# A linear-attention and MLP kernel on one core: the low part of the weights made by an accumulating DMA, and the plan's costs and start times set anew

## The chip, the cores and the metric

The kernel runs on one core of a Trainium2 chip. The metric is the device time of one execution in microseconds; before the change it is 558.08 us, the median of three runs (557.09 to 559.31). The core has five engines that run beside each other: TensorE (PE in the profile; its weight loads are shown apart as PEld), VectorE (DVE), ScalarE (ACT), GpSimd (POOL) and SyncE (SP), which here only issues DMAs. Each engine works through its own instructions in the order in which the program gives them.

## What is computed

```python
def _attn_ref(r, k, v, w, u):                    # B, H, S, D = 4, 8, 768, 48
    for t in range(S):
        cur = np.einsum('bhd,bhe->bhde', u[None] * kt, vt)
        y[:, :, t] = np.einsum('bhd,bhde->bhe', rt, state + cur)
        state = wt[:, :, :, None] * state + np.einsum('bhd,bhe->bhde', kt, vt)

def _moe_ref(x, w_in, w_out):                    # 3072 tokens, 384 -> 2048 -> 384
    h = x @ w_in
    g = np.where(h > 0.0, h, np.exp(np.minimum(h, 0.0)) - 1.0)
    return g @ w_out
```

A recurrent attention over 768 time steps, for 4 batches and 8 heads, feeds an MLP with an ELU between its two products. The MLP's weights are given in float64; the kernel gets them as pairs of 32-bit words.

## The kernel before

**Tiling.** Time is cut into 6 chunks of 128 steps. A *unit* is one chunk of one batch: 24 units, numbered i = 4 x chunk + batch. The MLP of a chunk takes its 4 units together, 512 columns, and goes through 16 *steps* f of 128 hidden columns each.

**A unit's attention.** Loads of w, k, r, v (L338) and, from unit 8 on, rk; two scans on DVE (es L344, gs L354); products r_hat and k_hat on DVE (L358, L361); the diagonal (by TensorE and ACT for the first 8 units, pd L385 and md L389, then am L396; by POOL and DVE for the others, L368, L371, L375, L403); the scores on TensorE (s, L413), masked by DVE (mk, L416); the value pass on TensorE (v, L443, tile pa_y), which needs the state; its result is split into a high and a low part, xh on ACT (L449) and xl on DVE (L453). For the next chunk's state the unit's k is transposed (t, L421), copied (kt, L425), multiplied with v (u, L460, tile pa_u) and added to the state by DVE (up, L468).

**A weight step.** For each f, two loads of 384 KB (w_in and w_out, L482) go to a raw buffer. ACT scales the upper words into a buffer wg (a, L487); DVE clears bits of the upper words (cand, L495) and merges both words into wg (cb L499, cc L503): wg now holds the weights in float32. ACT rounds them to the high part w_h (wh, L506), and DVE subtracts w_h from wg to get the low part w_l (wl, L509). There are two wg buffers, so the a of step f + 2 waits for the wl of step f. All 16 steps are converted once and stay in SBUF for all chunks.

**The MLP of a step.** Each product is the sum of three: w_h with xh, w_h with xl, w_l with xh. g1 is 9 matmuls (L227 to L229, three of each kind), then Relu and Exp on ACT (r1 L233, r2 L236), ELU on DVE (stt, L239), the split into gh (ACT, L243) and gl (DVE, L247), and g2, 9 matmuls into three accumulators (L256 to L258). A step may be cut into two half steps of 256 columns: for the first FH[c] steps of a chunk, the halves for batches 0 and 1 come first, then the halves for batches 2 and 3, and then the whole steps. After a chunk, its result is copied out and stored (L269, L270).

**The order.** A planner written out in the kernel (class Plan) makes the order of all engines' instructions. Each piece of work has an engine, an assumed cost (COST), what it must come after, and the buffers that it takes (SLOTS, hold). Backward from due times each gets a latest time ("late"); forward, a model of the engines picks, whenever an engine is free, the ready piece with the smallest latest time. The due times come from BEGINS, the assumed beginning of each chunk's MLP: step n of chunk c has its time t at BEGINS[c] + n x pace, with pace = (BEGINS[c+1] - BEGINS[c]) / 16; its g1 is due at t + 2.12 and its g2 at t + 2 x pace + 2.12. A buffer that is taken (three slots each for k, r and v, for four units of a chunk) holds a load back, but does not move the latest time of the work that frees it. A chunk's loads may not be planned before BEGINS[c] - LEAD. Only the order goes to the chip, where semaphores keep the dependences; the assumed costs do not.

Of the kernel before, what the change touches and what calls it, by code (L numbers as in the profile page):

```python
# [19 lines left out]
P = 128  # L20
# [12 lines left out]
FH = (6, 6)  # L33
# [23 lines left out]
def WLE(f):  # L57
    return "DVE"
# [15 lines left out]
class Plan:  # L74
# [15 lines left out]
    def order(self):  # L90
# [23 lines left out]
        ready = {e: [] for e in ("PE", "DVE", "ACT", "POOL", "SP")}  # L114
# [5 lines left out]
        server = 0.0  # L120
# [5 lines left out]
        while len(order) < len(ts):  # L126
            moved = False
            for e in ready:
# [33 lines left out]
                end = now + t["dur"]  # L162
                busy[e] = end
# [48 lines left out]
def mlp(nc, w_h, w_l, ps_acc, ps_h, ml, po, dst, last=False):  # L212
# [49 lines left out]
    def out(m):  # L262
# [13 lines left out]
def rwkv_elu_kernel(ctx, tc, wkr, rk, vp, u, uz, gkrw, gv, gu, w_in, w_out, out):  # L276
# [207 lines left out]
    def conv_a(f):  # L484
        g = stg.tile([P, 2, NK, P], U32, tag="wg", name="wg", bufs=2)
# [24 lines left out]

    def guard():
# [17 lines left out]
    for u_ in units:  # L529
        i, c, b = u_["i"], u_["c"], u_["b"]  # L530
        early = max(0.0, BEGINS[c] - LEAD) if c > 0 else 0.0
        for n, kb in (("w", 232), ("k", 229), ("r", 229), ("rk", 393), ("v", 262)):
            if n == "rk" and i < ND:
                continue
# [8 lines left out]
        if i < ND:  # L543
# [4 lines left out]
            add(("md", i), "ACT", K["md"], lambda u_=u_: diag_out(u_), [("pd", i)])  # L548
            add(("sp", i), "ACT", K["spa"], lambda u_=u_: spread_act(u_), [("md", i), ("const",)])
        else:  # L550
            e1, e2 = ENG(i)
            for n, e, fn, dep in (("rk", e1, r_k, [("ld_rk", i)]), ("rku", e2, r_k_u, [("rk", i), ("ub",)])):
                add((n, i), e, K[n if e == "DVE" else "p" + n],
                    lambda u_=u_, fn=fn, e=e: fn(u_, nc.vector if e == "DVE" else nc.gpsimd), dep, lock=True)
            add(("dg", i), "DVE", K["dg"], lambda u_=u_: diag(u_), [("rku", i)])
            add(("sp", i), "POOL", K["sp"], lambda u_=u_: spread(u_), [("dg", i)], lock=True)
# [16 lines left out]
    for f in range(NF):  # L573
# [10 lines left out]
        e = WLE(f)  # L584
        add(("wl", f), e, K["wl" if e == "DVE" else "pwl"], lambda f=f, e=e: conv_l(f, nc.vector if e == "DVE" else nc.gpsimd), [("wh", f)], lock=True)
# [29 lines left out]
    for u_ in units:  # L615
        i, c = u_["i"], u_["c"]
        for n, users in dict(w=["es", "gs"], k=["s", "t"], r=["s", "v"], rk=["dg"], v=["v", "u"]).items():
            hold(n, ("ld_" + n, i), [(x, i) for x in (users if n != "k" else users + ["kh"])])
        hold("eg", ("es", i), [("fl", i), ("rh", i), ("kh", i)] + [("pc", i)] * (c > 0))
        hold("md", ("md", i) if i < ND else ("dg", i), [("sp", i)])  # L620
        if i < ND:
# [16 lines left out]
    add(("guard",), "PE", 0.3, guard, [("fl", i) for i in range(NU)], due=BEGINS[-1] + 20)  # L638
# [127 lines left out]
```

## Time and profile before

| | us |
|---|---|
| median of three runs | 558.08 |
| the profiled execution | 556.87 |
| its span, first to last instruction | 554.8 |
| TensorE busy | 519.8 |
| DVE busy | 362.5 |
| ACT busy | 285.6 |
| POOL busy | 69.9 |

The page of the profile gives, for one execution, the busy time of each engine, the span in 40 equal slices (a digit is the busy share in tenths), and groups of instructions by line, with their count, busy time, mean duration in ns, and the idle time of the engine before them with what ended it. PEclk is the share of TensorE's full clock that the chip granted. Other views used here are a table of stretches (length, then the busy time of each engine with its instruction count, the granted clock, the DMA engines' busy share and GB/s), the chain of work that ended last in order of time, the waits of an engine for another, and the instructions in order of time. Matmuls overlap in the profile, so that the sum over groups is more than TensorE's busy time.

### The profile page before, as it was taken

Reading aid. Unit: us, or ns where it says so; the run is one execution under the profiler, and the core shown is the slowest. Engines: PE = TensorE matmul, PEld = TensorE weight load, DVE = VectorE, ACT = ScalarE, POOL = GpSimd, SP = SyncE. Lnnn points to the kernel's source line nnn. Section 1 sums busy time; section 2 is a strip of 40 time slices with the busy share of each in tenths; the row PEclk is TensorE's granted clock in tenths of the full one; section 3 lists DMA queues with packets and bytes.
Section 4 is the critical chain, followed back from the end, with each engine's and each line's share of the span. In section 5 each row is a group of like instructions: output and inputs, shape, how many; then the busy total and the mean of one; then the engine's idle time right before and its main releaser. Section 6 shows DMA issues by size and latency. Waiting matters only on the chain.

```text
span 554.8 us, 10007 instructions
## 1 busy us (share of the span) xinstructions
PE 519.8 (94%) x4065; PEld 430.3 (78%) x4065; DVE 362.5 (65%) x565; ACT 285.6 (51%) x558; POOL 69.9 (13%) x72
## 2 busy tenths in 40 slices
PE   5875999999999999999999999998799999999993
PEld 5765898889998887787878788876578878888882
DVE  6899999998796375369377335987596345333331
ACT  3668587687665443455443445643274432534441
POOL 1000000000240011215002300704530001000000
PEclk9977999999999999999999999999699999999998
DMA  8863574034410036211036200226520011100001
GB/s 267 250 199 120 156 234 168 1 87 144 122 60 2 0 90 192 59 55 36 0 91 201 69 0 18 74 91 209 153 70 1 0 37 38 58 0 1 0 1 61
DMA packets 26739, 47.36 MB, mean 85 GB/s; under 512 B 2752, under 2 KB 9280, under 8 KB 26688
## 3 DMA queue, kind: packets, MB, share of 16 engines
q1 hardware_dynamic: 26688, 46.66, 27.3%
q8 instruction: 34, 0.56, 0.4%
q14 instruction: 17, 0.14, 0.1%
HBM read 41.93 MB, written 4.72 MB: 84 GB/s over the span
## 4 chain that ended last, share of the span: by engine, by line
PE 83%; DVE 7%; DMA 3%; issue 3%; ACT 2%; SPq 1%; DVEq 0%; ACTq 0%
PE acc L256 12%; PE ph L227 12%; PE ph L229 11%; PE ph L228 11%; PE acc L257 11%; PE acc L258 11%; PE pa_y L443 6%; PE pa_s L413 4%; PE pa_u L460 2%; DMA v<-in_vp_dram 1%; PE pa_d L385 1%; PE pa_t L421 1%; DMA ubd<-in_uz_dram 1%; DVE gl L247 1%; DVE am L416 1%
## 5 line engine op out<-in xcount | busy, mean ns | idle before, releaser
L239 DVE SCALAR_TENSOR_TENSOR m<-m,ph 128x512 f32<-128x512 f32 (+1 forms) x108 | 67.1, 624 | 106.2 <-ACT m L236 105.9
L227 PE MATMUL ph<-xh,w_h 128*128 128x512 f32 (+1 forms) x324 | 123.2, 380 | 3.6 <-ACT w_h L506 1.6
L233 ACT ACTIVATE m<-ph 128x512 f32<-128x512 f32 (+1 forms) x108 | 59.3, 549 | 124.0 <-PE ph L229 120.8
L229 PE MATMUL ph<-xh,w_l 128*128 128x512 f32 (+1 forms) x324 | 121.0, 373 | 1.9 <-DVE w_l L509 1.9
L256 PE MATMUL acc<-gh,w_h 128*128 128x512 f32 (+1 forms) x325 | 122.0, 375 | 0.0
L228 PE MATMUL ph<-xl,w_h 128*128 128x512 f32 (+1 forms) x324 | 121.1, 374 | 0.2
L257 PE MATMUL acc<-gl,w_h 128*128 128x512 f32 (+1 forms) x325 | 120.2, 370 | 0.0
L258 PE MATMUL acc<-gh,w_l 128*128 128x512 f32 (+1 forms) x325 | 120.0, 369 | 0.0
L247 DVE TENSOR_TENSOR gl<-m,gh 128x512 fp32r<-128x512 f32 (+1 forms) x108 | 70.8, 658 | 35.1 <-ACT gh L243 34.8
L243 ACT CAST gh<-m 128x512 fp32r<-128x512 f32 (+1 forms) x108 | 61.4, 570 | 49.9 <-DVE m L239 43.4
L227 PEld LDWEIGHTS ph<-xh,w_h 128*128 128x128 f32 x324 | 62.2, 192 | 17.8 <-DVE m L239 3.0
L229 PEld LDWEIGHTS ph<-xh,w_l 128*128 128x128 f32 x324 | 62.1, 192 | 13.4 <-DVE w_l L509 2.4
L256 PEld LDWEIGHTS acc<-gh,w_h 128*128 128x128 f32 x325 | 61.4, 189 | 12.7 <-issue 1.0
L228 PEld LDWEIGHTS ph<-xl,w_h 128*128 128x128 f32 x324 | 62.3, 192 | 11.4 <-DVE xl L453 0.8
L258 PEld LDWEIGHTS acc<-gh,w_l 128*128 128x128 f32 x325 | 61.4, 189 | 11.3
L257 PEld LDWEIGHTS acc<-gl,w_h 128*128 128x128 f32 x325 | 61.4, 189 | 11.3 <-DVE gl L247 0.3
L236 ACT ACTIVATE m<-m 128x512 f32<-128x512 f32 (+1 forms) x108 | 63.1, 584 | 3.1
L403 POOL TENSOR_SCALAR_AFFINE_SELECT am<-md 128x512 f32<-128x512 f32 x32 | 29.2, 934 | 221.7 <-PE pa_y L443 156.2
L416 DVE COPY_PREDICATED am<-upper,pa_s 128x512 f32<-128x512 uint32 x48 | 32.8, 737 | 13.0 <-PE pa_s L413 11.9
L368 POOL TENSOR_TENSOR rk<-rk 128x384 f32<-128x384 f32 x16 | 18.3, 1147 | 171.9 <-DMA rk<-in_rk_dram 171.9
L413 PE MATMUL pa_s<-r,k 48*128 48x128 f32 x384 | 31.9, 304 | 7.7 <-issue 6.4
L413 PEld LDWEIGHTS pa_s<-r,k 48*128 48x128 f32 x384 | 26.9, 204 | 13.4 <-issue 9.9
(61 smaller groups left out, 504.4 us busy)
## 6 DMA issues: line engine op xcount, KB each, us to landing
v<-in_vp_dram SPq DMA_DIRECT2D x24, 256.0 KB, 3.1
rk<-in_rk_dram SPq DMA_DIRECT2D x16, 384.0 KB, 3.7
w<-in_wkr_dram SPq DMA_DIRECT2D x24, 226.2 KB, 4.8
k<-in_wkr_dram SPq DMA_DIRECT2D x24, 224.0 KB, 3.1
r<-in_wkr_dram SPq DMA_DIRECT2D x24, 224.0 KB, 5.1
out_dram<-o SPq DMA_DIRECT2D x17, 256.0 KB, 2.1
wrawx<-in_w_in_dram SPq DMA_DIRECT2D x10, 384.0 KB, 3.9
wrawx<-in_w_out_dram SPq DMA_DIRECT2D x10, 384.0 KB, 4.5
```

Source lines behind the costliest of these rows:

```text
L227: nc.tensor.matmul(ph, w_h[:, f, 0, k], xh[:, k, :], start=(k == 0), stop=False)
L228: nc.tensor.matmul(ph, w_h[:, f, 0, k], xl[:, k, :], start=False, stop=False)
L229: nc.tensor.matmul(ph, w_l[:, f, 0, k], xh[:, k, :], start=False, stop=(k == NK - 1))
L233: act(s["m"], s["ph"], AF.Relu, scale=-1.0)
L236: act(s["m"], s["m"], AF.Exp, scale=-1.0)
L239: stt_(s["m"], s["m"], -1.0, s["ph"], ALU.add, ALU.max)
L243: nc.scalar.copy(s["gh"], s["m"])
L247: nc.vector.tensor_tensor(s["gl"], s["m"], s["gh"].bitcast(F32), ALU.subtract)
L256: nc.tensor.matmul(a_, w_h[:, f, 1, m], s["gh"][:, s_], start=(f == 0 and lo == 0), stop=False)
L257: nc.tensor.matmul(a_, w_h[:, f, 1, m], s["gl"][:, s_], start=False, stop=False)
L258: nc.tensor.matmul(a_, w_l[:, f, 1, m], s["gh"][:, s_], start=False, stop=(f == NF - 1 and q == parts - 1))
L413: nc.tensor.matmul(pa[q][:, p], u_["k"][rs, p, :], u_["r"][rs, p, :], start=True, stop=True)
```

## The change

The low part of a weight step was wg - w_h on DVE. For the 12 steps in WLD, ACT now writes the negated, rounded wg into w_l (conv_n), and a DMA issued from POOL's queue adds wg to it in place (conv_d). Steps 0, 8, 11 and 15 keep DVE's subtraction. In the plan, the landing is a piece of work of its own on an assumed engine NET, with 4.0 us (WDL). A wg buffer is now held until w_l has landed and w_h is written.

The plan's other inputs change too. COST has new values. BEGINS and LEAD are new. FH was 6, 6 (half steps in chunks 0 and 1) and is now 4, 5, 0, 5. On TensorE the model adds 0.2 us (SWITCH) where the kind of work changes, and 3.9 us (STAY) to the latest time of work that would change between the kinds in MODES (s, v, u, pd) and all others. Each value pass of a chunk comes after the one of the batch before it. One of the two halves of the last output is issued from ACT's queue. The rest renames (DIAG and SPREAD say which engine makes the diagonal, as ND and ENG did, with the same assignment).

```diff
-FH = (6, 6)
+FH = (4, 5, 0, 5, 0, 0)
...
-COST = dict(es=1.5, gs=1.4, pc=0.2, pd=0.6, md=0.22, spa=2.4, rh=0.62, kh=0.62, rk=0.48, rku=0.48, prk=1.1, prku=1.1, dg=0.5, mk=0.7, up=0.7, sc=0.5, xl=0.48,
-            cand=0.5, cv=0.9, wl=0.9, pwl=1.9, stt=0.6, gl=0.64, fl=1.4, kt=0.5, xh=0.46, a=0.87, wh=0.8, r1=0.58, r2=0.6, gh=0.6,
-            sp=1.7, s=1.15, t=0.5, v=1.75, v0=1.1, u=0.5, g=2.12, out=0.6)
+COST = dict(es=1.2, gs=1.45, rh=0.61, kh=0.61, rk=0.48, rku=0.48, prk=1.0, prku=1.1, dg=0.47, mk=0.64, up=0.73, sc=0.47, xl=0.48,
+            pc=0.1, pd=0.45, md=0.1, spa=2.35, cand=0.5, cv=0.87, wl=0.87, pwl=1.9, wn=0.73, wd=1.0, stt=0.6, gl=0.6, fl=1.16, kt=0.43,
+            xh=0.43, a=0.81, wh=0.73, r1=0.56, r2=0.54, gh=0.52, sp=1.57, s=0.88, t=0.37, v=1.55, v0=0.9, u=0.37, g=2.1, out=0.5)
...
-BEGINS = (20.6, 125.1, 205.2, 299.0, 400.1, 445.7, 557.5)
+BEGINS = (19.3, 145.5, 209.8, 321.6, 420.1, 430.6, 535.4)
 SOON = 0.0
-LEAD = 70.0
-ND = 8
+STAY = 3.9
+SWITCH = 0.2
+MODES = dict(s=1, v=2, u=3, pd=4)
+WLD = (1, 2, 3, 4, 5, 6, 7, 9, 10, 12, 13, 14)
+WDL = 4.0
+LEAD = 96.4
+DIAG = ["PE"] * 8 + ["POOL"] * 16
+SPREAD = ["ACT"] * 8 + ["POOL"] * 16
...
-                    u = (t["late"], rank[k])
+                    u = (t["late"] + (STAY if e == "PE" and (k[0] in MODES) != (mode in MODES) else 0.0), rank[k])
...
                 end = now + t["dur"]
+                if e == "PE":
+                    end += SWITCH * (MODES.get(mode, 0) != MODES.get(k[0], 0))
+                    mode = k[0]
...
-            nc.sync.dma_start(dst[m * P:(m + 1) * P, s_], o[:, m, s_])
+            (nc.scalar if last and m == NK - 1 and q == 0 else nc.sync).dma_start(dst[m * P:(m + 1) * P, s_], o[:, m, s_])
...
+    def conv_n(f):
+        act(w_l[:, f], raws[f][1].bitcast(F32), AF.Copy, scale=-1.0)
+
+    def conv_d(f):
+        nc.gpsimd.dma_start(w_l[:, f].bitcast(F32), raws[f][1].bitcast(F32), accum_op=ALU.add)
...
+        if b:
+            after.append(("v", i - 1))
         add(("v", i), "PE", K["v" if c else "v0"], lambda u_=u_: value(u_), after)
...
-        e = WLE(f)
-        add(("wl", f), e, K["wl" if e == "DVE" else "pwl"], lambda f=f, e=e: conv_l(f, nc.vector if e == "DVE" else nc.gpsimd), [("wh", f)], lock=True)
+        if f in WLD:
+            add(("wn", f), "ACT", K["wn"], lambda f=f: conv_n(f), [("cc", f)])
+            add(("wd", f), "POOL", K["wd"], lambda f=f: conv_d(f), [("wn", f)])
+            add(("wl", f), "NET", WDL, lambda: None, [("wd", f)])
+        else:
+            add(("wl", f), "DVE", K["wl"], lambda f=f: conv_l(f, nc.vector), [("wh", f)], lock=True)
...
-        hold("wg", ("a", f), [("wl", f)])
+        hold("wg", ("a", f), [("wl", f), ("wh", f)])
...
-    add(("guard",), "PE", 0.3, guard, [("fl", i) for i in range(NU)], due=BEGINS[-1] + 20)
+    add(("guard",), "PE", 0.3, guard, [("fl", i) for i in range(NU)], due=BEGINS[-2] + 15)
```

More of the change, by code (lines that the diff above doesn't have):

```diff
@@ L113, in order @@
         free = lambda p, n: not any(ring[p][1][(ring[p][0] + x) % len(ring[p][1])] for x in range(n))
-        ready = {e: [] for e in ("PE", "DVE", "ACT", "POOL", "SP")}
+        ready = {e: [] for e in ("PE", "DVE", "ACT", "POOL", "SP", "NET")}
         count = {k: len(t["after"]) for k, t in ts.items()}
@@ L119, in order @@
         locked = {"DVE": 0.0, "POOL": 0.0}
-        server = 0.0
+        server, mode = 0.0, None
         turn = {p: list(q) for p, q in self.queue.items()}
@@ L548, in rwkv_elu_kernel @@
             add(("md", i), "ACT", K["md"], lambda u_=u_: diag_out(u_), [("pd", i)])
+        else:
+            e = DIAG[i]
+            for n, fn, dep in (("rk", r_k, [("ld_rk", i)]), ("rku", r_k_u, [("rk", i), ("ub",)])):
+                add((n, i), e, K[n if e == "DVE" else "p" + n],
+                    lambda u_=u_, fn=fn, e=e: fn(u_, nc.vector if e == "DVE" else nc.gpsimd), dep, lock=True)
+            add(("md", i), "DVE", K["dg"], lambda u_=u_: diag(u_), [("rku", i)])
+        if SPREAD[i] == "ACT":
             add(("sp", i), "ACT", K["spa"], lambda u_=u_: spread_act(u_), [("md", i), ("const",)])
         else:
[L551 to L556, printed above, removed]
+            add(("sp", i), "POOL", K["sp"], lambda u_=u_: spread(u_), [("md", i)], lock=True)
         add(("s", i), "PE", K["s"], lambda u_=u_: score(u_), [("rh", i), ("kh", i), ("sp", i)])
@@ L616, in rwkv_elu_kernel @@
         i, c = u_["i"], u_["c"]
-        for n, users in dict(w=["es", "gs"], k=["s", "t"], r=["s", "v"], rk=["dg"], v=["v", "u"]).items():
+        for n, users in dict(w=["es", "gs"], k=["s", "t"], r=["s", "v"], rk=["md"], v=["v", "u"]).items():
             hold(n, ("ld_" + n, i), [(x, i) for x in (users if n != "k" else users + ["kh"])])
         hold("eg", ("es", i), [("fl", i), ("rh", i), ("kh", i)] + [("pc", i)] * (c > 0))
-        hold("md", ("md", i) if i < ND else ("dg", i), [("sp", i)])
-        if i < ND:
+        hold("md", ("md", i), [("sp", i)])
+        if DIAG[i] == "PE":
             hold("rk", ("rkc", i), [("pd", i)])
```

9 lines of the change are left out of this document (4 added, 5 removed).

## The prediction

> **What bounds the kernel now.** I read the page's shares and slices first, then a table of stretches, then the waits and the order of time inside the bad stretches.
>
> ```profile
> span 554.8 us, 10007 instructions
> PE 519.8 (94%) x4065; PEld 430.3 (78%) x4065; DVE 362.5 (65%) x565; ACT 285.6 (51%) x558; POOL 69.9 (13%) x72
> ...
> PE   5875999999999999999999999998799999999993
> ...
> DVE  6899999998796375369377335987596345333331
> ...
> PEclk9977999999999999999999999999699999999998
> ```
>
> TensorE is the bound almost everywhere; two dents stand in its row (slices 1 to 4, and 27 and 28), and both have a dent in the granted clock. The first lies where DVE is at 9. The table of stretches gives sizes (busy us and instruction count by engine, then clock, DMA share, GB/s):
>
> ```profile
> 0.00:20.00 20.00, 13.84 (x80) 12.76 (x84) 14.50 (x24) 10.89 (x27) 2.31 (x8) 1.00 0.95 284
> 20.00:70.00 50.00, 38.65 (x410) 34.30 (x403) 46.19 (x76) 32.86 (x73) 0.00 (x0) 0.86 0.52 167
> 70.00:110.00 40.00, 40.00 (x205) 33.82 (x204) 39.47 (x59) 29.21 (x48) 0.00 (x0) 1.00 0.40 134
> ...
> 160.00:376.00 216.00, 214.21 (x1625) 172.40 (x1629) 136.15 (x209) 103.17 (x185) 35.80 (x33) 1.00 0.22 65
> 376.00:400.00 24.00, 18.43 (x272) 14.44 (x265) 14.55 (x24) 5.77 (x12) 11.43 (x11) 0.79 0.64 198
> 400.00:545.00 145.00, 145.00 (x898) 117.05 (x898) 67.46 (x102) 67.76 (x117) 8.66 (x9) 1.00 0.07 21
> ```
>
> Two stretches lose time. 20 to 70 us: 11.4 us of idle TensorE and 0.14 x 50 = 7.0 us of withheld clock, 18.4 in all, with DVE busy 46.2 of 50. 376 to 400 us: 5.6 idle and 0.21 x 24 = 5.0 clock, 10.6 in all, with no engine full. Elsewhere TensorE is busy throughout, so work taken from DVE after 70 us buys nothing by itself.
>
> The first loss. The chain passes through DVE here; its longest hole is put down to "issue", but DVE's own rows (the first and last of them here) run through it without a gap, because the third and fourth batch's scans and products must be done before the next scores:
>
> ```profile
> 43.92 6.38 issue
> ...
> 41.98 2.35 DVE L344 TENSOR_TENSOR_SCAN eg<-w,reset 112x516 f32<-112x516 f32 x2
> 44.25 0.93 DVE L499 SCALAR_TENSOR_TENSOR wg<-wg,wrawx 128x768 uint32<-128x768 uint32 x1
> 45.21 0.96 DVE L503 SCALAR_TENSOR_TENSOR wg<-wrawx,wg 128x768 uint32<-128x768 uint32 x1
> ...
> 50.12 0.68 DVE L358 TENSOR_TENSOR r<-r,eg 112x512 f32<-112x512 f32 x1
> ```
>
> So in this stretch a microsecond off DVE is about a microsecond off the path.
>
> The second loss is loads that come late for unit 19, the last of chunk 4:
>
> ```profile
> 377.95 0.60 PE L421 MATMUL pa_t<-ident,k 112*128 112x112 f32 x4
> 378.59 2.87 DMA k<-in_wkr_dram
> 382.00 0.56 PE L460 MATMUL pa_u<-v,kt 128*48 128x48 f32 x16
> 383.85 0.63 SPq L338 DMA_DIRECT2D v<-in_vp_dram  x1
> 391.39 1.94 PE L443 MATMUL pa_y<-am,v 128*32 128x128 f32 x32 [4.34 <-DMA v<-in_vp_dram]
> ```
>
> k and v have three slots for four units of a chunk. k(19) may load only after the transpose of unit 16 (378), v(19) only after its outer product (382); both were issued the moment the slot came free, and v then took 7.5 us among other loads. TensorE stood, and the clock fell to half after it.
>
> **The change part by part.** The weight step's prices:
>
> ```profile
> L509 DVE TENSOR_TENSOR w_l<-wg,w_h 128x768 fp32r<-128x768 f32 x16 | 15.2, 951 | 0.2
> L506 ACT CAST w_h<-wg 128x768 fp32r<-128x768 f32 x16 | 13.3, 829 | 1.6 <-DVE wg L503 1.6
> L499 DVE SCALAR_TENSOR_TENSOR wg<-wg,wrawx 128x768 uint32<-128x768 uint32 x10 | 9.5, 953 | 0.2
> L503 DVE SCALAR_TENSOR_TENSOR wg<-wrawx,wg 128x768 uint32<-128x768 uint32 x10 | 9.5, 952 | 0.1
> L487 ACT ACTIVATE wg<-wrawx 128x768 f32<-128x768 f32 x10 | 9.1, 914 | 1.6 <-DVE w_l L509 1.3
> L495 DVE TENSOR_SCALAR wrawx<-wrawx 128x768 uint32<-128x768 uint32 x10 | 5.5, 553 | 0.0
> L247 DVE TENSOR_TENSOR gl<-m,gh 128x512 fp32r<-128x512 f32 x84 | 58.8, 700 | 33.6 <-ACT gh L243 33.4
> L247 DVE TENSOR_TENSOR gl<-m,gh 128x256 fp32r<-128x256 f32 x24 | 12.0, 514 | 1.5 <-ACT gh L243 1.4
> L239 DVE SCALAR_TENSOR_TENSOR m<-m,ph 128x512 f32<-128x512 f32 x84 | 57.4, 684 | 102.6 <-ACT m L236 102.5
> L239 DVE SCALAR_TENSOR_TENSOR m<-m,ph 128x256 f32<-128x256 f32 x24 | 9.7, 412 | 3.7 <-ACT m L236 3.5
> ```
>
> 1. *DVE's subtraction goes for 12 steps*: 12 x 0.951 = 11.4 us. Only those before TensorE fills count: steps 1 to 6 (28.99 to 62.97 us below), 6 x 0.951 = 5.7. Two half-step pairs fewer in chunk 0 take 2 x (2 x 0.926 - 1.384) = 0.9 more off DVE. Sum 6.6. Against it, the low part arrives later in the first burst, where TensorE already waits for it. I take **-6.0**; ends: 0 (the wait only changes its name) and -12 (all 11.4 and some clock).
>
> 2. *Added on ACT*: 12 copies, nearest row the cast at 0.829, 10 us. ACT is busy 32.9 of 50, so they fit in its holes; 0.
>
> 3. *Added on POOL and the DMA engines*: 12 issues and 12 transfers of 384 KB. No row shows an accumulating transfer. POOL is empty from 20 to 110, so an issue waits for nobody. Nearest rows:
>
> ```profile
> DMA to landing us min/median/max: 3.4/4.3/8.1
> ...
> ACT wg L487 <- DVE w_l L509: 3.7, 4, 1.3
> ...
> 28.99 0.95 DVE L509 TENSOR_TENSOR w_l<-wg,w_h 128x768 fp32r<-128x768 f32 x1
> ...
> 62.97 0.96 DVE L509 TENSOR_TENSOR w_l<-wg,w_h 128x768 fp32r<-128x768 f32 x1
> ...
> 109.11 0.93 DVE L509 TENSOR_TENSOR w_l<-wg,w_h 128x768 fp32r<-128x768 f32 x1
> ```
>
> The first is the weight loads' time to land, also 384 KB each. An addition reads two sources, so it lands between 3.4 and twice 8.1 us; I take 5, and 1 for the issue (SP's issue of v, above, took 0.63): T = 6 from the negated copy to the landing. What it can hold up is the two wg buffers, on which ACT already waits (second row). One turn of a buffer was 0.914 + 0.553 + 0.953 + 0.952 + 0.829 + 0.951 = 5.15 us; with the DMA it is 3.37 + 0.83 + 0.83 + T = 5.03 + T = 11. The odd steps have six DMA turns and two of DVE: 40.5 + 6T. From step 1's start at 17.9 us, T = 6 gives 94 us for the last weights, against 110 before. So T is hidden; cover ends at T = 8.6. Cost **0**; ends 0 and +50 (T = 1 + 16.2: 160 us).
>
> The trace shows that the AND of 768 elements takes 553 ns where the others need 952: a doubled rate. By the Trainium skill (SBUF — State Buffer, section "SBUF: two separate sides") a DMA issued from GpSimd cannot write its descriptors while DVE is in a mode of two ports. It speaks against this change; by it T grows by an estimated 0.55 at most, to 6.55, which leaves the sum as it is; no run here shows such a DMA.
>
> 4. *The loads of chunk 4*. By the plan's arithmetic, the order key of unit 16's transpose was 440.3 (from 445.7 back through unit 20's chain), behind chunk 3's last g2 at 299 + 15 x 6.32 + 12.6 + 2.1 = 408.6: it ran when nothing else was left. Now chunk 5 begins at 430.6 and each value pass waits for the one before, so the key is about 421, u's 422, while chunk 3's last g2 stands at 321.6 + 15 x 6.16 + 12.3 + 2.1 = 428.4. Even with the 3.9 for a change of kind, u comes ahead of it. k(19) and v(19) get their slots while products remain to be done. And chunk 5's loads may now start at 334 instead of 376, out of that jam. I take **-9.0** of the 10.6; ends -10.6 and +3.
>
> 5. *Grouping on TensorE* (STAY). Two value passes in one run took 3.20 us, one alone 1.67:
>
> ```profile
> 119.55 1.67 PE pa_y L443 x56
> ...
> 143.16 3.20 PE pa_y L443 x112
> ```
>
> 0.14 for a joined pair; with some 40 joins possible at most -5.6. Some are joined already: **-1.5**; other end +2, a product that starts later. Half steps in chunk 3 cost TensorE nothing (256 columns stream in half the time), DVE 5 x 0.47 = 2.3 where it has room.
>
> 6. *Last output on ACT's queue*: one SP issue off the tail, **-0.5**; ends -0.7 and 0.
>
> Sum: -6.0 - 9.0 - 1.5 - 0.5 = -17.0; span 537.8. The profiled execution took 556.87, 2.1 more than its span, and the median of the runs is 1.2 above it: 537.8 + 2.1 + 1.2 = 541.1. I say **541**.
>
> **The rivals.**
> *The late load stays* (or another chunk's fourth unit gets one): the three slots are unchanged, and the keys only order what is ready. No 9.0: 541 + 9 = 550.
> *The startup is not DVE's sum but its order*: the low part of steps 1 to 4 is later by some 4 us, TensorE waits for DMA where it waited for DVE, and the 6.0 go: 547.
> *Neither*: only grouping and tail are left: 556, no change.
> *Slower: the buffers' turns.* If an accumulating transfer takes T over 8.6 us, the wg chain is longer than before, 6 us for each microsecond. At T = 12 the last weights come 20 us later; TensorE can put chunk 1's attention in between (its four value passes alone, 4 x 1.67, are 6.7), so I count 11 of them lost, and the 6.0 too: 541 + 17 = 558, as before. That is the point from which it decides; at T = 13, a transfer of one and a half of the slowest load, it is 564. For it: the DMA engines are 0.52 busy in that stretch, one plain load took 8.1, and the buffers already make ACT wait. Against it: the median of 4.3 under the same load.
>
> **How the numbers follow.** Forecast 0.47; late load stays 0.21; startup not gained 0.11; neither 0.08; slower 0.13. Over 0.5%, about what a measurement of this kernel can tell from no change, is 2.8 us: faster 0.79, same 0.08, slower 0.13. Low end: the larger ends of 1 and 4 with most of 5, 541 - 11 = 530. High end: to take in "neither", 557. Left out are the slow transfer and a little below 530.
>
> **What would show it.** Right: no L509 for steps 1 to 7; DVE below 44 of 50 from 20 to 70, clock above 0.9; transfers landing in 4 to 6 us; no wait of pa_y for v, clock 1.0 around chunk 4. Wrong: ACT's wg waiting for a DMA for several us at a time; ph at L229 waiting for DMA; a dent in the clock after 350 us; POOL's issues stretching DVE's rows.

## The result and the profile after

| | before | after |
|---|---|---|
| median of 16 runs each, us | 557.34 | 564.07 |
| lowest and highest, us | 554.99 to 559.31 | 559.92 to 569.97 |
| profiled execution and its span, us | 556.87, 554.8 | 560.90, 558.6 |

The ratio of the runs is 1.0113, with a 95% interval of 1.0092 to 1.0134; it leaves out after's two slowest runs (568.52 and 569.97), which count as a slower state of the kernel. The change makes the kernel **1.1% slower**, where 541 us was forecast. The profiled execution of after lies at the low end of its runs, 3.2 us under their median. So the profile explains 3.8 us of span; the rest of the 6.7 is a spread over the runs that one trace does not show.

In the changed file the MLP's and the attention's lines stand 5 lower (ph L232 to L234, acc L261 to L263); the three ways to a low part are L514 (DVE), L517 (ACT's negated copy) and L520 (POOL's DMA). From the page after:

```profile
span 558.6 us, 10096 instructions
...
PE 523.1 (94%) x4101; PEld 431.2 (77%) x4101; DVE 352.3 (63%) x557; ACT 295.5 (53%) x576; POOL 75.3 (13%) x84
...
PE   6759899899999999999899999999999999999994
...
DVE  6897589898863248449935543699994337333231
...
w_l<-wg POOLq DMA_DIRECT2D x12, 384.0 KB, 6.4
```

DVE has 10.2 us less to do (352.3 against 362.5), as the change intends, and the second dent in TensorE's row, at slices 27 and 28, is gone. But the first dent has grown: before it ended with slice 4, and now it reaches to slice 8. The last line is the new transfer, with 6.4 us from issue to landing (median of 12). The table of stretches after has the same columns as before (TensorE, its weight loads, DVE, ACT, POOL with counts; clock; DMA share; GB/s):

```profile
20.00:70.00 50.00, 39.25 (x370) 34.93 (x371) 38.96 (x67) 35.85 (x78) 5.32 (x6) 0.81 0.70 189
70.00:110.00 40.00, 36.85 (x183) 28.21 (x182) 35.43 (x52) 33.87 (x67) 3.64 (x5) 0.95 0.78 216
160.00:376.00 216.00, 210.83 (x1657) 172.57 (x1656) 125.57 (x200) 101.54 (x192) 34.67 (x34) 1.00 0.23 66
376.00:400.00 24.00, 23.38 (x361) 19.25 (x360) 22.87 (x38) 10.32 (x21) 12.14 (x14) 1.00 0.53 158
```

Row by row against before: DVE falls from 46.2 to 39.0 of 50 in the first stretch, yet TensorE does fewer instructions there (370 against 410). From 70 to 110 TensorE was never idle; now it is for 3.2 us at a clock of 0.95. From 160 to 376 it idled 1.8 us and now 5.2. Only the fourth row is better: 23.38 busy at full clock, against 18.43 at 0.79.

**A measure for all runs.** The clock column cannot be compared between runs, since in some traces the clock's records begin only 24 or 35 us into the span. So I use the *loss* of a stretch: its length less the time that its matmuls take at full speed. An MLP matmul of 512 columns counts 0.2315 us (the distance at which they follow each other where TensorE is full; half of it for 256 columns), a score pass 1.09, a value pass 1.67 (0.95 for the four of chunk 0, which have 32 of its 56 matmuls), an outer product 0.49, a transpose 0.39, a diagonal 0.84. In every trace below these add up to 400.0 + 87.7 us, so the losses add up to the span less 487.7, and what one stretch gains can be set against what another gives back. A loss is idle time, withheld clock, or matmuls that follow each other more slowly than counted:

| loss, us | 20-120 | 120-360 | 360-400 | 400-540 | after 540 | all |
|---|---|---|---|---|---|---|
| before | 22.1 | 7.2 | 11.1 | 1.2 | 9.9 | 67.1 |
| after | 28.8 | 14.2 | 2.2 | 1.6 | 8.2 | 70.9 |
| difference | +6.7 | +7.0 | -8.9 | +0.4 | -1.7 | +3.8 |

(The first 20 us lose 15.5 and 15.8.) The late loads gave what was forecast, the tail some more. The start of the kernel and the chunk changes between 120 and 360 us took back more.

What TensorE waited for between 20 and 120 us in after (line, releaser: us in total, times, longest):

```profile
PE acc L261 <- ACT gh L248: 8.1, 2, 5.4
PE ph L234 <- DMA w_l<-wg: 2.3, 2, 1.2
```

Of the two waits for ACT's gh, the one of 5.4 us is there without landings too (first experiment below); the other, 2.7 us at 67.6, follows from a landing. ACT's queue just ahead of it:

```profile
66.35 0.89 ACT L492 ACTIVATE wg<-wrawx 128x768 f32<-128x768 f32 x1 [4.05 <-DMA w_l<-wg]
67.14 0.39 ACT L248 CAST gh<-m 128x256 fp32r<-128x256 f32 x1
```

The cast that TensorE needs stood behind a conv_a (L492), which waited 4.05 us for a transfer to land in its buffer.

### The profile page after: what moved, and what is told of

The parts are those of the page before. It is cut to its first block, busy times and chain, and to the rows that moved or that the text cites. A ratio compares the mean times of both kernels' runs of the same rounds, so it can differ in the third digit from the quotient of the medians.

```text
span 558.6 us, 10096 instructions
## 1 busy us (share of the span) xinstructions
PE 523.1 (94%) x4101; PEld 431.2 (77%) x4101; DVE 352.3 (63%) x557; ACT 295.5 (53%) x576; POOL 75.3 (13%) x84
## 4 chain that ended last, share of the span: by engine, by line
PE 68%; DVE 10%; DMA 9%; issue 6%; ACT 5%; SPq 1%; POOL 0%; DVEq 0%; ACTq 0%; POOLq 0%
PE acc L262 10%; PE acc L261 10%; PE ph L232 10%; PE ph L233 9%; PE acc L263 9%; PE ph L234 9%; PE pa_y L448 6%; PE pa_s L418 3%; DMA r<-in_wkr_dram 2%; DMA w_l<-wg 2%; DMA k<-in_wkr_dram 2%; DVE m L244 1%; DMA wrawx<-in_w_out_dram 1%; DVE eg L349 1%; DVE am L421 1%
## 5 line engine op out<-in xcount | busy, mean ns | idle before, releaser
L244 DVE SCALAR_TENSOR_TENSOR m<-m,ph 128x512 f32<-128x512 f32 (+1 forms) x110 | 67.4, 615 | 107.0 <-ACT m L241 106.7
L261 PE MATMUL acc<-gh,w_h 128*128 128x512 f32 (+1 forms) x331 | 123.9, 374 | 8.1 <-ACT gh L248 8.1
L232 PE MATMUL ph<-xh,w_h 128*128 128x512 f32 (+1 forms) x330 | 124.3, 377 | 2.5 <-DVE m L244 2.0
L234 PE MATMUL ph<-xh,w_l 128*128 128x512 f32 (+1 forms) x330 | 121.3, 368 | 3.7 <-DMA w_l<-wg 2.3
L262 PE MATMUL acc<-gl,w_h 128*128 128x512 f32 (+1 forms) x331 | 122.9, 371 | 1.5 <-DVE gl L252 1.4
L233 PE MATMUL ph<-xl,w_h 128*128 128x512 f32 (+1 forms) x330 | 122.5, 371 | 0.2
L263 PE MATMUL acc<-gh,w_l 128*128 128x512 f32 (+1 forms) x331 | 121.4, 367 | 0.0
L261 PEld LDWEIGHTS acc<-gh,w_h 128*128 128x128 f32 x331 | 63.0, 190 | 20.9 <-ACT gh L248 8.4
L232 PEld LDWEIGHTS ph<-xh,w_h 128*128 128x128 f32 x330 | 62.8, 190 | 16.2 <-DVE m L244 3.4
L234 PEld LDWEIGHTS ph<-xh,w_l 128*128 128x128 f32 x330 | 63.0, 191 | 15.8 <-DMA w_l<-wg 2.9
L262 PEld LDWEIGHTS acc<-gl,w_h 128*128 128x128 f32 x331 | 63.0, 190 | 14.9 <-DVE gl L252 4.5
L263 PEld LDWEIGHTS acc<-gh,w_l 128*128 128x128 f32 x331 | 63.1, 190 | 11.0
L408 POOL TENSOR_SCALAR_AFFINE_SELECT am<-md 128x512 f32<-128x512 f32 x32 | 24.7, 801 | 198.7 <-PE pa_y L448 174.4
L370 ACT ACTIVATE junk<-eg,lim 112x1032 bf16<-112x1032 f32 x24 | 27.6, 1152 | 16.1 <-DVE eg L359 16.1
L349 DVE TENSOR_TENSOR_SCAN eg<-w,reset 112x516 f32<-112x516 f32 x24 | 31.5, 1312 | 4.2 <-DMA w<-in_wkr_dram 4.2
```

The costliest lines, as they stand in the source:

```text
L232: nc.tensor.matmul(ph, w_h[:, f, 0, k], xh[:, k, :], start=(k == 0), stop=False)
L233: nc.tensor.matmul(ph, w_h[:, f, 0, k], xl[:, k, :], start=False, stop=False)
L234: nc.tensor.matmul(ph, w_l[:, f, 0, k], xh[:, k, :], start=False, stop=(k == NK - 1))
L244: stt_(s["m"], s["m"], -1.0, s["ph"], ALU.add, ALU.max)
L261: nc.tensor.matmul(a_, w_h[:, f, 1, m], s["gh"][:, s_], start=(f == 0 and lo == 0), stop=False)
L262: nc.tensor.matmul(a_, w_h[:, f, 1, m], s["gl"][:, s_], start=False, stop=False)
```

## The experiments

All ratios are to the runs of before on the same chip, with their 95% interval; losses come from each run's profile.

### At the changed kernel's own order: what is the landing worth?

Four kernels keep the changed kernel's order of all instructions and change only how the 12 low parts are made, so that no new plan blurs the comparison.

**No landing.** The copies stay, the DMAs go.

```diff
     def conv_d(f):
-        nc.gpsimd.dma_start(w_l[:, f].bitcast(F32), raws[f][1].bitcast(F32), accum_op=ALU.add)
+        pass
```

> The changed kernel in the same order, the 12 accumulating DMAs left out, so that the low part of those steps is only the negated high part. Turns theory: a wg buffer is free after ACT's copy, the loss from 20 to 120 falls by 7 us or more: 552 to 557 us. Order theory: 562 to 565, as with the DMA.

Measured: 554.38 us, ratio 0.994 (0.9911 to 0.997).

**DVE's subtraction in the same place.** Copy and DMA go; conv_l runs where the plan had the landing.

```diff
+        high, due = set(), set()
         for t in plan.order():
+            n, f = t["key"][0], t["key"][-1]
+            if n in ("wn", "wd"):
+                continue
             t["fn"]()
+            if n == "wh":
+                high.add(f)
+            if n == "wl" and f in WLD:
+                due.add(f)
+            for f in sorted(high & due):
+                conv_l(f, nc.vector)
+                due.discard(f)
```

> The changed kernel in the same order, with DVE's subtraction put where the landing stood in the order, for the same 12 steps; no copy on ACT, no DMA. If DVE's sum bounds the start (the step of the prediction that gave -6.0): 11 us of DVE come back, 560 to 566 us, the loss from 20 to 120 some 6 to 11 above the 22.4 of the run without landings. If the landing is the price and DVE's time is not on the path: 552 to 556.

Measured: 561.79 us, ratio 1.01 (1.0067 to 1.0133).

**A plain copy in place of the addition.**

```diff
-        nc.gpsimd.dma_start(w_l[:, f].bitcast(F32), raws[f][1].bitcast(F32), accum_op=ALU.add)
+        nc.gpsimd.dma_start(w_l[:, f].bitcast(F32), raws[f][1].bitcast(F32), accum_op=ALU.bypass)
```

> The changed kernel in the same order, the 12 DMAs copying over the negated high part in place of adding to it (so the low part is wrong: it is the full weight). Alone the copy took 2.6 us and the addition 4.0. If it is the length of the landing that counts: 558 to 561 us, between the kernel without landings (554.4) and the changed one (564.1). If it is any use of POOL's queue: 562 to 565.

Measured: 557.70 us, ratio 1.0019 (0.9992 to 1.0045).

**A third wg buffer**, with the junk tile made smaller to give it room.

```diff
-        junk = at.tile([R2, 2 * NP * CW], BF16, tag="junk", name="junk", bufs=1)
+        junk = at.tile([R2, 2 * NP * CW], mybir.dt.uint8, tag="junk", name="junk", bufs=1)
...
-        g = stg.tile([P, 2, NK, P], U32, tag="wg", name="wg", bufs=SLOTS["wg"])
+        g = stg.tile([P, 2, NK, P], U32, tag="wg", name="wg", bufs=3)
```

> The changed kernel in the same order, three wg buffers on the chip in place of two (the flag's unread output is made in 8 bits to make room). Turns theory: ACT's wg no longer waits for landings, 554 to 560 us. Order theory: 562 to 565.

Measured: 560.41 us, ratio 1.0081 (1.0058 to 1.0103).

| at the order of after | ratio | loss 20-120 | 120-360 | 360-400 |
|---|---|---|---|---|
| no landing | 0.9940 | 22.4 | 14.8 | 2.1 |
| plain copy | 1.0019 | 25.7 | 13.5 | 2.5 |
| adding DMA, three buffers | 1.0081 | 24.1 | 14.4 | 2.7 |
| DVE's subtraction | 1.0100 | 28.2 | 15.8 | 2.2 |
| adding DMA (after) | 1.0113 | 28.8 | 14.2 | 2.2 |

The profiles of after and of the three-buffer kernel are of runs 3 us under their medians, so their losses are low; the other three lie at theirs. Three things follow. First, with 557 us for before, taking the subtraction off DVE and putting the copies on ACT is worth 1.6%, 8.9 us (no landing against DVE's), and the landing takes back 1.73%, 9.6 us; the intervals leave 2 to 3 us on each. The exchange itself, +0.13%, is **nothing that can be measured** at this order. Second, the order alone (DVE's row) costs 1.0%, 5.6 us: it loses 6.1 us more than before at 20 to 120 and 8.6 at 120 to 360, and gains 8.9 at 360 to 400. The loss at 120 to 360 is there however the low part is made. Third, how long the landing takes is part of its price: the plain copy, which lands sooner, gives back 0.94%, 5.2 us. Its landings and those of the adding DMA (least, median, most), each from the answer for the tile w_l, after first:

```profile
DMA to landing us min/median/max: 3.9/6.4/8.3
```

```profile
DMA to landing us min/median/max: 2.6/5.0/7.9
```

The third buffer gains 0.3%, which the intervals don't separate from nothing.

### At the order of before: the exchange alone

Two kernels take before's order as it is. In the first, ACT writes the negated copy beside its cast and nothing more is done for the 12 low parts; in the second, POOL's adding DMA stands where DVE's subtraction stood.

```diff
...
         for t in plan.order():
+            n, f = t["key"][0], t["key"][-1]
+            if n in ("wh", "wl") and f in WLD:
+                conv_n(f) if n == "wh" else None
+                if n == "wl":
+                    continue
             t["fn"]()
```

(conv_n and conv_d are the changed kernel's.)

> Before's order, unchanged, but in the 12 steps DVE's subtraction is left out and ACT writes the negated high part beside its cast; nothing is added to it, so the low part is wrong in these steps. It measures term 1 (DVE's relief) alone, in the order of before. Theory A (in the first burst a microsecond off DVE is a microsecond off the path): 549 to 552, the loss at 20 to 120 falls from 22.0 to about 16. Rival B (what rules there is the order of the instructions in their queues, so that less work on DVE helps only where an order was planned for it): 555 to 558, the loss at 20 to 120 stays at 20 to 23.

Measured: 554.97 us, ratio 0.9969 (0.9949 to 0.9989); the loss at 20 to 120 is 21.2. So DVE's relief, with the copies on ACT, is worth 0.3%, 1.7 us, and not 6. DVE is at 41.9 of 50 where it was at 46.2:

```profile
20.00:70.00 50.00, 39.73 (x415) 35.66 (x415) 41.90 (x71) 38.34 (x83) 0.00 (x0) 0.83 0.55 171
```

What ended DVE's idle time between 20 and 70 us in this run (engine, line, releaser: us in total, times, longest), and the longest hole of TensorE in the chain of work:

```profile
DVE gl L248 <- ACT gh L244: 4.0, 6, 1.1
DVE m L240 <- ACT m L237: 2.3, 2, 1.8
```

```profile
43.04 6.31 issue
49.36 2.08 PE pa_s L414 x16
```

The hole ahead of the scores was 6.38 us before and is 6.31 now; it only begins 0.9 us earlier, though four subtractions (3.8 us) ahead of it are gone. DVE stands idle in their place, waiting for ACT: the elements of a half step go ACT, ACT, DVE, ACT, DVE in turn, and ACT now has the negated copies in its queue as well (busy 38.3 of 50 us, before 32.9). No kernel left out both the subtractions and the copies, so how much of the relief the copies took is not shown.

The second kernel differs from the first in one word:

```diff
-                conv_n(f) if n == "wh" else None
+                conv_n(f) if n == "wh" else conv_d(f)
```

> Before's order, unchanged, but in the 12 steps ACT writes the negated high part beside its cast, and where DVE's subtraction stood POOL issues the adding DMA: the change's exchange of DVE for DMA alone, without the new order. Theory A (the landing costs more than DVE's relief gives: at the changed kernel's order the two were +9.7 and -7.4, so +2.3 in sum): 557 to 566, landings of 5.5 to 7 us, the loss at 20 to 120 from 24 to 32. Rival B (the landing fits into an order that was not planned for it): 549 to 554. Rival C (an order made for a subtraction of 0.95 us has no room for a landing of 6): over 566.

Measured: 589.06 us, ratio 1.0578 (1.0553 to 1.0604); the loss at 20 to 120 is 49.6. Set against the kernel without a landing, the landings cost 6.1%, 34 us. Yet they are short here:

```profile
DMA to landing us min/median/max: 3.9/4.2/7.4
```

What the 4.2 us do is seen in ACT's own queue, in order of time (start, length, what ended the idle time before), with POOL's issues and one row of DVE:

```profile
36.12 0.90 ACT L488 ACTIVATE wg<-wraw 128x768 f32<-128x768 f32 x1 [6.16 <-issue]
36.94 0.83 ACT L513 ACTIVATE w_l<-wg 128x768 fp32r<-128x768 f32 x1
...
42.33 0.92 ACT L488 ACTIVATE wg<-wrawx 128x768 f32<-128x768 f32 x1 [2.82 <-DMA w_l<-wg]
...
44.53 0.83 ACT L513 ACTIVATE w_l<-wg 128x768 fp32r<-128x768 f32 x1
...
49.90 0.91 ACT L488 ACTIVATE wg<-wrawx 128x768 f32<-128x768 f32 x1 [3.19 <-issue]
...
52.05 0.83 ACT L513 ACTIVATE w_l<-wg 128x768 fp32r<-128x768 f32 x1
```

```profile
38.07 0.87 POOL L516 DMA_DIRECT2D w_l<-wg  x1 [7.50 <-ACT w_l L513]
45.66 0.85 POOL L516 DMA_DIRECT2D w_l<-wg  x1 [6.72 <-ACT w_l L513]
```

```profile
46.77 0.95 DVE L504 SCALAR_TENSOR_TENSOR wg<-wrawx,wg 128x768 uint32<-128x768 uint32 x1
```

L488 is conv_a of step 3, 4 and 5; L513 the negated copy of step 2, 3 and 4. The last two conv_a start at a landing (38.07 + 4.2 is 42.3; 45.66 + 4.2 is 49.9; the page puts the second down to "issue", but the landing ends there). Step 4 was merged by DVE at 47.7, so that its copy could run; but conv_a of step 5 stood ahead of it in ACT's queue, and that waited until 49.9 for the landing of step 3. The copy ran at 52.05, its landing came later with it, and so on. With a landing in the turn, an engine that works in order makes two buffers act like one: one step per 7.6 us (38.07 to 45.66).

### New plans for the same exchange

Three kernels let the planner make a new order. The first has the changed kernel's rules with all low parts on DVE (WLD empty), and late in chunk 5, where the DMA engines have little else to do, four transfers between the wg buffers as probes, adding and plain in turn. The second has before's rules and costs, with the 12 DMAs. The third tells the planner that a landing takes 8 us.

```diff
-WLD = (1, 2, 3, 4, 5, 6, 7, 9, 10, 12, 13, 14)
+WLD = ()
...
+    for j, (n_, op) in enumerate(((-8, ALU.add), (-7, ALU.bypass), (-6, ALU.add), (-5, ALU.bypass))):
+        add(("probe", j), "POOL", 1.0, lambda j=j, op=op: nc.gpsimd.dma_start(
+            raws[14 + j % 2][1].bitcast(F32), raws[15 - j % 2][1].bitcast(F32), accum_op=op), [("g2", len(seq) + n_)])
```

> The changed kernel's rules, costs and due times, but DVE makes the low part in all 16 steps (the plan is made again with that); late in chunk 5, while POOL and the DMA engines have nothing else, four transfers between the two wg buffers, which nothing reads any more, are added: accumulate, copy, accumulate, copy, 384 KB each. Turns theory (the landing holds the two wg buffers and starves TensorE from 20 to 120 us): about 557 us, the loss from 20 to 120 back at 22 or below from 29, the gap at 376 to 400 still gone. Order theory (the new order loses it, whatever makes the low part): 562 to 566. The accumulating transfer alone: 4 to 5 us to land if the 6.4 seen are contention, over 6 if that is its own price.

Measured: 566.16 us, ratio 1.0211 (1.0144 to 1.0277); losses 23.9 at 20 to 120, 19.0 at 120 to 360. The first two probes as issued on POOL:

```profile
480.44 1.00 POOL L635 DMA_DIRECT2D wg<-wg  x1
484.75 0.57 POOL L635 DMA_DIRECT2D wg<-wg  x1 [3.31 <-DMA wg<-wg]
```

```profile
DMA to landing us min/median/max: 2.6/3.3/5.3
```

The first adding transfer landed after 4.01 us, the two plain ones after 2.65 and 2.61. The second adding one took 5.32, beside three stores of the output that were issued from 485.7 us on. The time lies about where the second expectation put it: the new rules and due times lose without any landing.

```diff
...
+            add(("wn", f), "ACT", 0.8, lambda f=f: conv_n(f), [("cc", f)])
+            add(("wd", f), "POOL", 1.0, lambda f=f: conv_d(f), [("wn", f)])
+            add(("wl", f), "NET", WDL, lambda: None, [("wd", f)])
...
```

> The kernel before, its costs and due times, with the accumulating DMA for the same 12 steps as the only change. Turns theory: 7 us slower than before, about 564 us, with ACT's wg waiting for landings. Order theory: 552 to 558, no slower than before.

Measured: 577.45 us, ratio 1.037 (1.0344 to 1.0395); losses 34.0 and 16.7.

```diff
-WDL = 4.0
+WDL = 8.0
```

> The changed kernel, its plan told that a landing takes 8.0 us in place of 4.0 (the plan is made again; alone the transfer took 4.0 us, in the changed kernel 6.4). If a wrong figure in the plan is the cause, work is put where the landings leave room, and it comes to 555 to 559 us. If the wait for the wg buffers is the cause whatever the plan knows, 561 to 566.

Measured: 594.37 us, ratio 1.0686 (1.0653 to 1.0719); losses 40.2 and 29.1. A longer assumed landing, which should have left it more room, cost 5.7% against the changed kernel. So a kernel that was planned anew says little of a single part: one number moves every instruction behind it, and moves the time by more than the parts in question. The comparisons at a fixed order carry the verdicts here.

### The loads of chunk 4

**The due time alone**: before, with chunk 5 assumed to begin at 410.6, so that the plan wants unit 16's transpose earlier.

```diff
-BEGINS = (20.6, 125.1, 205.2, 299.0, 400.1, 445.7, 557.5)
+BEGINS = (20.6, 125.1, 205.2, 299.0, 400.1, 410.6, 557.5)
```

> The kernel before, with one due time changed: chunk 5's MLP begins at 410.6 in the plan, not 445.7, so that the transpose and the outer product of unit 16 come ahead of chunk 3's last products. Due-time theory: the gap at 376 to 400 closes and the time falls by 7 to 9 us, 548 to 551. If it was the earlier loads or another rule of the change that closed it: 555 to 558.

Measured: 557.22 us, ratio 1.0005 (0.9982 to 1.0028); the loss at 360 to 400 stays at 11.1. The value pass hardly waits for v any more (0.2 us), but the new plan put chunk 4's scans and products into one block on DVE, and TensorE waits for DVE instead (5.8 us at once):

```profile
PE acc L257 <- DVE gl L247: 5.8, 1, 5.8
```

**The late instructions alone**: before's own order with six instructions moved.

```diff
-        for t in plan.order():
+        todo = plan.order()
+        moved = {("up", 15): [("t", 16), ("kt", 16), ("ld_k", 19)], ("v", 17): [("u", 16), ("up", 16), ("ld_v", 19)]}
+        by = {t["key"]: t for t in todo}
+        late = [k for ks in moved.values() for k in ks]
+        for t in todo:
+            if t["key"] in late:
+                continue
             t["fn"]()
+            for k in moved.get(t["key"], ()):
+                by[k]["fn"]()
```

> Before's own order of instructions, with six of them moved: unit 16's transpose, its copy and the load of k(19) stand right behind unit 15's state update, and unit 16's outer product, state update and the load of v(19) right behind unit 17's value pass (in before they came behind unit 17's value pass and unit 18's scores). The weight steps are before's, all subtractions on DVE. Theory A (the loss of 10.6 us at 376 to 400 is the late slot of unit 19's k and v, so that moving the two slot releases ahead takes it out without any new plan): 548 to 552, the loss in 360 to 400 falls from 11.1 to under 5. Rival B (the loss only moves, as when the due time alone was changed and TensorE then waited for DVE at 367 to 380): 555 to 558, the loss between 360 and 400 stays at 8 to 11.

Measured: 553.08 us, ratio 0.9951 (0.9931 to 0.9972); the loss at 360 to 400 falls from 11.1 to 7.4. That is between the two expectations. The stretch of the gap in this run:

```profile
376.00:400.00 24.00, 20.19 (x346) 16.91 (x346) 17.53 (x29) 8.13 (x17) 10.66 (x12) 1.00 0.62 200
```

The clock stays at 1.00 (0.79 before), and no wait for v is left; 3.8 us of idle time remain, in short waits for a mask, a copy and the split of an MLP step; 2.1 more, a wait for a state update, stand at 373.

**The same with the last output's issue on ACT's queue**, by the changed kernel's line for it:

```diff
-            nc.sync.dma_start(dst[m * P:(m + 1) * P, s_], o[:, m, s_])
+            (nc.scalar if last and m == NK - 1 and q == 0 else nc.sync).dma_start(dst[m * P:(m + 1) * P, s_], o[:, m, s_])
```

> The kernel with the six moved instructions, and besides it the last output's issue on ACT's queue as in the change (term 6 alone, on top of the moved loads). If term 6 has its forecast size: 0.5 us below the kernel with the moved instructions, so 547.5 to 551.5, within 0 to -0.7 of it; if the shorter tail of the changed kernel (8.2 against 9.8) is this issue alone: 1.0 to 1.6 below it.

Measured: 552.47 us, ratio 0.9917 (0.9894 to 0.9941). The loss after 540 us is 7.8, against 9.0 without this line and 9.9 before. The medians are 0.6 us apart, the ratios 0.34%, and the two intervals overlap a little: the sign is fairly sure, the size is not. This kernel is the fastest of those that do the whole computation: 0.8% faster than before and 1.9% faster than the changed one (0.9917 / 1.0113), with DVE's subtractions as they were.

## Why the prediction was wrong

Its terms, with what the runs showed for each:

| step | forecast | shown |
|---|---|---|
| 1, 2. DVE relieved, copies on ACT | -6.0, 0 | -1.7 at before's order, -8.9 at after's; not measured apart |
| 3. landing | 0 | +9.6 at after's order, +34 at before's |
| 4. loads of chunk 4 | -9.0 | -8.9 of loss |
| 5. grouping on TensorE | -1.5 | not measured alone; the new order: +7.0 of loss at 120 to 360 |
| the new order from 20 to 120 | no term | +6.1 of loss, with DVE's subtraction |
| 6. last output | -0.5 | -0.6 by the medians, -1.2 of loss |

The change forecast was -17.0 us and the measured one is 1.13% of 557, +6.3. Steps 1 to 3, the exchange, were to give 6.0 and cost 0.7; the order's part (steps 4 to 6) was to give 11.0 and cost 5.6 (DVE's row). So 16.6 of the 23.3 us between them lie with the order and 6.7 with the exchange.

**Step 3 failed, and not by the size of T.** I took T = 6 us from the negated copy to the landing, with cover up to 8.6. The landing took 6.4 at the median from its issue, and the issue followed the copy by some 0.3: 6.7, inside the cover by my own reckoning. What failed is the turn of a buffer. I summed the durations of its six instructions, 5.15 us before and 5.03 + T after, as though each began when the last ended. Before's own trace spoke against that. The rows of conv_a (count, least/median/most ns, first and last start) give steps 1 to 15 from 17.9 to 99.6 us:

```profile
L487 ACT ACTIVATE wg<-wrawx x10: 894/914/935, 17.9 to 93.7; 128x768 f32<-128x768 f32 x10
L487 ACT ACTIVATE wg<-wraw x6: 876/904/919, 10.1 to 99.6; 128x768 f32<-128x768 f32 x6
```

Steps 1 and 15 share a buffer, seven turns apart: 81.7 / 7 = 11.7 us a turn, more than twice the sum. The rest is time spent in ACT's and DVE's queues behind other work. The changed kernel's rows:

```profile
L492 ACT ACTIVATE wg<-wrawx x10: 892/909/915, 17.6 to 111.6; 128x768 f32<-128x768 f32 x10
L492 ACT ACTIVATE wg<-wraw x6: 879/892/933, 9.4 to 115.2; 128x768 f32<-128x768 f32 x6
```

(115.2 - 17.6) / 7 = 13.9 us a turn. How much of that the landing makes shows in the same two rows of the kernels that differ in the low part alone (conv_a of step 1, of step 15, and a turn in us):

| low parts | at the order of before | at the order of after |
|---|---|---|
| DVE's subtraction | 17.9, 99.6: 11.7 | 19.6, 115.0: 13.6 |
| copy, no landing | 18.5, 98.8: 11.5 | 18.8, 109.1: 12.9 |
| copy and adding DMA | 18.5, 133.0: 16.4 | 17.6, 115.2: 13.9 |

At before's order nothing of the landing is hidden: it makes a turn 4.9 us longer, where issue and landing take 4.5, and seven such turns are the 34 us that this kernel loses. At after's order a turn hides most of it, and 1.0 us comes through, 7 us in seven turns, of the 9.6 that the landing costs there. So my zero was wrong at both orders, and how wrong depends on the order. The step from 11.7 to 13.6 has no landing in it: it is the new order's, for which my sum had no term. The last low part began at 120.3 us in the changed kernel, where I forecast the last weights for 94 and the kernel before had them at 110, and it began no sooner with DVE's subtraction in its place:

```profile
L514 DVE TENSOR_TENSOR w_l<-wg,w_h x4: 948/949/958, 28.0 to 120.3; 128x768 fp32r<-128x768 f32 x4
```

```profile
L514 DVE TENSOR_TENSOR w_l<-wg,w_h x16: 931/951/959, 26.9 to 122.0; 128x768 fp32r<-128x768 f32 x16
```

One thing that the changed kernel's order does differently is seen on POOL. It sends two transfers close behind each other, each for one buffer; that this is why it hides more of the landing was not tried:

```profile
37.40 0.86 POOL L520 DMA_DIRECT2D w_l<-wg  x1 [13.02 <-ACT w_l L517]
38.85 0.85 POOL L520 DMA_DIRECT2D w_l<-wg  x1 [0.59 <-ACT gh L248]
```

The transfers are slower there (6.4 at the median against 4.2), with a DMA share of 0.70 from 20 to 70 us and 0.72 from 70 to 120, where the kernel with landings at before's order had 0.60 and 0.61. My rival on the slower side had this place and these buffers, at 558, but let T alone decide.

**Step 1's premise did not hold at the order from which I read it.** "In this stretch a microsecond off DVE is about a microsecond off the path": 4.3 us less of DVE work between 20 and 70 us moved the loss at 20 to 120 by 0.9. The end of 0 that I kept, "the wait only changes its name", is near what happened: DVE now waits for ACT. Part of that can be step 2's zero, since ACT had the copies to do. At after's order the relief is worth 8.9, but that order with DVE's subtraction loses 28.2 at 20 to 120 and without landing 22.4, against 22.1 before: the relief only pays for what the order spends. That is my rival "the startup is not DVE's sum but its order", with the engine that is waited for named wrongly: TensorE waits for ACT (8.1 us) more than for a DMA (2.3).

**Step 5's stretch went the other way.** I counted joined passes and gave +2 as the worst. Of the 7.0 us that 120 to 360 loses more, 3.4 are idle time of TensorE (busy 234.65 of 240 us, before 238.05). The kernels with other low parts at the same order lose as much there, so it is the order's. At one place where TensorE waits, DVE's work for the attention stands in one block and the MLP's own element waits behind it; DVE and POOL in order of time:

```profile
261.01 1.62 DVE L359 TENSOR_TENSOR_SCAN eg<-w,reset 112x516 f32<-112x516 f32 x1
262.55 0.66 DVE L252 TENSOR_TENSOR gl<-m,gh 128x512 fp32r<-128x512 f32 x1
263.13 1.50 DVE L363 TENSOR_TENSOR r<-r,eg 112x512 f32<-112x512 f32 x1
264.56 1.50 DVE L366 TENSOR_TENSOR k<-k,eg 112x512 f32<-112x512 f32 x1
265.98 2.65 DVE L433 TENSOR_TENSOR st<-st,pc 112x384 f32<-112x384 f32 x2
268.55 1.22 DVE L349 TENSOR_TENSOR_SCAN eg<-w,reset 112x516 f32<-112x516 f32 x1
269.69 0.66 DVE L244 SCALAR_TENSOR_TENSOR m<-m,ph 128x512 f32<-128x512 f32 x1
```

```profile
261.51 2.58 POOL L373 TENSOR_TENSOR rk<-rk 128x384 f32<-128x384 f32 x1
```

DVE's L244, which TensorE needs, runs at 269.69 behind 6.5 us of chunk 3's work; TensorE waits 1.6 us for it, of a loss of 1.9 in these 20 us. The two products L363 and L366 take 1.50 us each here, beside POOL's work, and 0.69 without it (last section): their 1.6 us more would about make up this wait, so the block alone need not be its cause. The changes to chunk 2 (200 to 240 us) and chunk 3 (300 to 340; 280 to 320 before) lose 4.4 and 4.6 us, where they lost 2.2 and 1.7; that is most of the 7.0. TensorE's waits between 120 and 360 us are all for DVE and ACT:

```profile
PE ph L232 <- DVE m L244: 2.0, 2, 1.6
PE pa_u L465 <- ACT kt L430: 1.3, 2, 0.7
PE acc L262 <- DVE gl L252: 0.9, 3, 0.6
```

The other 3.6 us are no idle time: matmuls follow each other more slowly than counted. By their starts in the trace, those of 256 columns are, beyond the idle time, 3.9 us late in sum in this stretch, against 1.2 before, and chunk 3 has them only now. I had put its half steps at nothing for TensorE; what slows them is not shown. Which of STAY, BEGINS, the half steps and the order of the value passes makes the rest was not tried one by one, and the new plans show that it could hardly be: that stays open.

**Step 4 was right** in place and size: the loss there went from 11.1 to 2.2. Of its cause a part is shown. The moved instructions give 3.7 of the 8.9 by the late slots alone, and the due time alone gave nothing; what in the new plan gives the other 5.2 was not tried, so that the whole size came may be luck. **Step 6** was right in sign.

Of the signs named beforehand, DVE below 44 of 50 and no wait for v came true; the clock above 0.9 from 20 to 70 did not (0.81), nor landings of 4 to 6 us (3.9 to 8.3). Two signs of being wrong came: TensorE waiting for a landing in ph (2.3 us, shown above), and ACT waiting for one in conv_a, 4.1 us at once:

```profile
ACT wg L492 <- DMA w_l<-wg: 4.9, 2, 4.1
```

The rule of the Trainium skill that I weighed (SBUF — State Buffer, section "SBUF: two separate sides") is that a DMA issued from GpSimd waits for DVE's two-port mode to write its descriptors. In the changed kernel no AND of DVE, the instruction that I took for that mode, ran beside any of the 12 issues, so their 0.85 to 1.02 us say nothing of it. In two of the other plans one began 0.53 and 0.59 us into an issue, and those issues took 1.17 and 1.24 us. This one is from the kernel with before's rules and the DMAs:

```profile
92.81 1.17 POOL L515 DMA_DIRECT2D w_l<-wg  x1 [22.80 <-ACT w_l L512]
```

```profile
93.34 0.56 DVE L495 TENSOR_SCALAR wrawx<-wrawx 128x768 uint32<-128x768 uint32 x1
```

The issue ended at 93.98, just behind the AND (93.90); in the plan with a landing of 8 us it was 75.19 behind 75.10. The other issues of these two kernels took 0.85 to 0.87, the first of each 1.01 and 1.02; one of 0.87 had an AND that began 0.71 us into it. So these two issues agree with the rule, at a price of 0.3 to 0.4 us each, and in the changed kernel it had no occasion.

## What to carry to other kernels

Measure the turn of a buffer from its first to its last use in the trace, not from the sum of its instructions: the difference is queueing, and how much of an added latency it hides depends on the order. Here all of 4.5 us came through at one order and 1.0 of 6.7 at the other. Before taking work off a busy engine, leave it out at the unchanged order and look at who waits then; busy for 46 of 50 us did not show that it set the pace. And where a planner makes the order, compare at a fixed order, since a changed plan moves the time by more than the change.

## What the runs showed of the hardware

An adding DMA of 384 KB inside SBUF costs more than a plain one: 4.01 us to landing against 2.65 and 2.61 with next to nothing beside it (5.32 beside stores of the output), and its issue holds POOL for 0.86 to 1.00 us against 0.56 and 0.57. Beside the weight loads both grow, to medians of 6.4 and 5.0.

DVE and POOL slow each other: DVE's product of 112x512 took 1.50 us while POOL's products ran, as quoted above, and 0.69 in the next unit without them:

```profile
275.52 0.69 DVE L363 TENSOR_TENSOR r<-r,eg 112x512 f32<-112x512 f32 x1
```

POOL's took 2.58 us where its median (least/median/most ns) is 1.02:

```profile
L373 POOL TENSOR_TENSOR rk<-rk x16: 1003/1021/2577, 134.3 to 398.1; 128x384 f32<-128x384 f32 x16
```

The Trainium skill (SBUF — State Buffer, section "Who interferes with whom") says that a DVE instruction with two inputs in SBUF contends with a GpSimd instruction that reads SBUF; the trace agrees. The plan keeps these two apart by locks, but by its assumed times, and on the chip they met.
